# One core, five engines, one hand-sized list: a new order of work for a GateLoop block and a maxout FFN

## The chip, the cores and the metric

The kernel runs on one core of a Trainium2 chip, in one launch. A core has five engines that run side by side, each through its own stream of instructions in order: PE multiplies matrices (the profile lists its weight loads apart, as PEld), DVE works on vectors, ACT computes functions such as exp and sin, POOL does odd jobs and issues some of the transfers, SP only issues transfers. Matrix products land in PSUM, everything else lives in SBUF. The metric is device time in microseconds (us), less is better.

## The reference

Two blocks follow each other. The first is a gated linear recurrence for 4 batches, 8 heads, 768 steps and head dimension 48; the second a feed-forward block on 3072 tokens, width 384, inner width 768:

```python
mag = np.sqrt(a_re * a_re + a_im * a_im)
scale = np.minimum(mag, 0.999) / (mag + 1e-06)
a_re_n, a_im_n = (a_re * scale, a_im * scale)
for t in range(S):
    new_re = ar * S_re - ai * S_im        # ar, ai: row t of a_re_n, a_im_n
    new_im = ar * S_im + ai * S_re
    S_re, S_im = (new_re + outer(k[t], v[t]), new_im)
    y[t] = q[t] @ S_re
x = y.transpose(0, 2, 1, 3).reshape(B * S, H * D)
h = np.maximum(np.maximum(x @ w1, x @ w2), x @ w3)
out = h @ w_out
```

## The kernel before

**Tiling.** The recurrence is not run step by step. It is cut into chunks of 128 steps; a chunk of one batch is one x, and two batches side by side (x and y in the names) make one group g. Six chunks a batch and four batches give 12 groups, 24 x's. Inside a chunk the product of all gates between two steps is written with logarithms of magnitudes (running sums of Ln) and with angles (running sums of turns), so the chunk becomes a masked product of q and k, and a state is carried from chunk to chunk.

**The words.** All work is cut into named words such as `tpqx:8`: the name is the step, x or y the half of the group, the number the group. On PE these are: `cs` and `sums` (running sums of angles and logs), `F` (decays), `tpk` and `tpq` (transposes of k and q), `A` and `B` (scores of a chunk), `dk` (update of the state), `y` (output of the chunk), all of them made of small matmuls; then the FFN: `U` (up projections, x @ (w2 - w1) and x @ (w3 - w1), 9 matmuls of 256 columns), and `P1` to `P7`, `Px`, `Py` (down projection by Strassen's scheme, 7 half-size products instead of 8, and the x @ w1 part folded into one matrix). An f32 matmul is two passes on PE, and each pass is a weight load and a matmul, so one `A` is 128 PE instructions, one `y` 224, one `B` or `F` 64, one `dk` 128, one `U` 36, one `P` 16. On the other engines: gate steps (`sqr`, `add`, `lnL`, `expw`, `lnw`, `mulw`, `turn` and others), angles (`t`, `nf`, `af`, `sa`, `sb`), the products with exp of the sums (`mk`, `uk`, `kEn`, `Q1`, `Q2`, `KB`, `QB`, `QG`), masks (`g0` to `g3`, `b0`, `b1`), state (`h0` to `h3`), and for the FFN `u`, `S1` to `S4`, `r` and `o`. `L...` words are loads, `D` the store.

**Start of the kernel.** The weights come as f64 words and are turned into f32 by hand: `WL` loads a block (12 blocks), `Wa` runs on ACT, `Wb`, `Wc`, `We`, `Wf` on DVE, and `Wg` adds the first weight matrix into a block of the others by an accumulating transfer that POOL issues. `T`, `t`, `M`, `m` fold w1 with w_out. `CL` builds constants (masks) on POOL. The first group's FFN runs in smaller words (`U11x` and so on), before the Strassen factors (`J`) exist.

**What sets the order.** One list, SCHEDULE (line 21), names all 1903 words in the order in which they are issued; a class `Bound` (line 202) ties every instruction of an engine to the one before it on that engine, so the list is the order of each engine. SP and POOL queues get their transfers in the same order. What crosses engines waits on semaphores. SLOTS gives, for each new tile of PSUM, one of four slots of two banks: a PE word that takes a slot waits until the slot's last tile has been read. OTHER names the words that change engine: a load in it goes by POOL's queue instead of SP's, a copy or an absolute value by DVE instead of ACT (`copy` line 242, `magnitude` line 249), and an addition by DVE instead of an accumulating transfer by POOL (`increase` line 256).

**Buffers.** The gate tiles L, w and e of a group have one buffer each; `gates` (line 504) takes all three at the group's first gate word. The result tiles `ot` (line 921) of both halves are taken together at the first of the words that add up results.

Of the kernel before, what the change touches and what calls it, by code (L numbers as in the profile page):

```python
# [31 lines left out]
say:0 atan:1 Wb4:0 Wc2:0 Wg1:0 kEnx:0 Wc4:0 We2:0 Lry:2 Lrx:2 sby:0 sqr:2 g2x:0 sqi:2 M0:0 Wf2:0 WL5:0 M1:0 add:2
uqy:0 lnL:2 expe:2 Bx:0 g3x:0 b0x:0 M2:0 b1x:0 tpqy:0 Qcy:0 m1:0 We4:0 Cdy:0 turn:1 sumsx:1 Eqx:1 uky:0 Wf4:0
tpky:0 Ekx:1 Wg2:0 csy:1 m0:0 Q2y:0 kEny:0 Enx:1 Kcy:0 Q1y:0 mqx:1 ty:1 dkx:0 sumsy:1 h1x:0 h2x:0 nfy:1 relu:2
csx:1 tx:1 mkx:1 QGx:0 Wa5:0 Eqy:1 nfx:1 Eky:1 expw:2 Lvy:0 dky:0 Ay:0 h1y:0 Wb5:0 abs:2 QBy:0 h3x:0 Wc5:0 g0y:0
Liy:3 KBy:0 g1y:0 We5:0 Z2:0 g2y:0 yx:0 g3y:0 WL7:0 Wa7:0 Wb7:0 Eny:1 Wf5:0 xx:0 lne:2 xor:2 Wg4:0 By:0 b0y:0 QGy:0
U11x:0 u11x:0 b1y:0 Fx:1 U01x:0 Z4:0 Wc7:0 half:2 f0x:1 f2x:1 f1x:1 f3x:1 We7:0 addw:2 lnw:2 expL:2 mulai:2 mulw:2
Wf7:0 yy:0 Z3:0 xy:0 u01x:0 U02x:0 h2y:0 h3y:0 Wg5:0 U12y:0 Lqy:1 Lvx:1 Lky:1 afy:1 say:1 U12x:0 stt:2 afx:1 u02x:0
sby:1 WL8:0 u12x:0 Wa8:0 Wb8:0 U11y:0 U01y:0 Cdy:1 Cdx:1 Wg7:0 sbx:1 atan:2 turn:2 Wc8:0 U02y:0 u01y:0 Fy:1 u11y:0
mqy:1 sax:1 f2y:1 f3y:1 f0y:1 f1y:1 We8:0 Wf8:0 u12y:0 u02y:0 U21y:0 csx:2 Lnop:2 tx:2 u21y:0 csy:2 ty:2 uqx:1  # L40
ukx:1 nfx:2 tpqx:1 Qcx:1 Lvx:2 uqy:1 nfy:2 sumsy:2 tpkx:1 Kcx:1 mky:1 Wg8:0 uky:1 tpqy:1 U22y:0 Qcy:1 Lqy:2 kEnx:1
tpky:1 Kcy:1 u22y:0 kEny:1 sumsx:2 Ekx:2 Lkx:2 Q1x:1 mkx:2 Eqy:2 dkx:1 Liy:4 afx:2 Q2x:1 Enx:2 Eky:2 mqy:2 sbx:2
sax:2 QBx:1 Q1y:1 h0x:1 Eny:2 Q2y:1 Oy:0 oy:0 h1x:1 KBx:1 h2x:1 h3x:1 Ax:1 Bx:1 g0x:1 g1x:1 g2x:1 g3x:1 QGx:1 Lqx:2
Lvy:2 Eqx:2 U21x:0 Fx:2 b0x:1 Ay:1 mqx:2 b1x:1 u21x:0 ukx:2 yx:1 U22x:0 Lix:3 sqi:3 f3x:2 f2x:2 J3:0 h0y:1 f1x:2
QBy:1 f0x:2 Lry:3 Lrx:3 sqr:3 add:3 lnL:3 expe:3 relu:3 lne:3 g0y:1 KBy:1 g1y:1 Lvy:1 Lky:2 mky:2 u22x:0 g2y:1
h0x:2 expw:3 abs:3 xx:1 Ox:0 ox:0 QGy:1 g3y:1 By:1 b0y:1 dky:1 b1y:1 uqx:2 addw:3 afy:2 h1y:1 Fy:2 tpkx:2 Kcx:2
h2y:1 h3y:1 f0y:2 xor:3 kEnx:2 Lnop:3 sumsx:3 Lix:4 f3y:2 tpqx:2 Qcx:2 lnw:3 Q1x:2 QBx:2 yy:1 xy:1 f2y:2 dkx:2
Lkx:3 h1x:2 KBx:2 h2x:2 h3x:2 f1y:2 Lqx:3 expL:3 mulw:3 half:3 QGx:2 Enx:3 Lvy:3 Eqx:3 Q2x:2 mulai:3 Ekx:3 Lry:4
U11:1 u11:1 mkx:3 stt:3 Cdy:2 atan:3 U12:1 mqx:3 u12:1 Ax:2 Bx:2 Fx:3 g0x:2 g1x:2 g2x:2 sqi:4 Lrx:4 sqr:4 Lix:5
say:2 g3x:2 Cdx:2 sby:2 U01:1 f3x:3 f2x:3 u01:1 f0x:3 uqy:2 f1x:3 U02:1 Lvx:3 b1x:2 add:4 lnL:4 S3:1 b0x:2 expe:4  # L50
uky:2 turn:3 h0x:3 h0y:2 J1:0 J2:0 tpky:2 Dx:0 Lky:3 u02:1 S1:1 kEny:2 S2:1 Kcy:2 tpqy:2 Qcy:2 yx:2 sumsy:3 xx:2
Lqy:3 Eny:3 Q2y:2 csy:3 Eky:3 ty:3 Eqy:3 nfy:3 csx:3 Q1y:2 tx:3 dky:2 nfx:3 h1y:2 lne:4 relu:4 Fy:3 afx:3 QBy:2
sbx:3 sax:3 h2y:2 J4:0 P5:1 QGy:2 Liy:5 h3y:2 KBy:2 f0y:3 f2y:3 P7:1 P1:1 Dy:0 Ay:2 f3y:3 f1y:3 By:2 P6:1 g0y:2
g1y:2 Px:1 g2y:2 S4:1 expw:4 r1:1 ukx:3 g3y:2 mqy:3 abs:4 P2:1 P3:1 b0y:2 b1y:2 yy:2 xy:2 uqx:3 tpqx:3 Lnop:4 r6:1
addw:4 r5:1 r7:1 r57:1 tpkx:3 kEnx:3 lnw:4 Qcx:3 Lry:5 mky:3 expL:4 Lkx:4 Q1x:3 mulw:4 afy:3 say:3 Kcx:3 sby:3 Py:1
P4:1 oy:1 ox:1 U11:2 u11:2 sumsx:4 Ekx:4 xor:4 Lrx:5 sqr:5 QBx:3 QGx:3 mulai:4 KBx:3 mkx:4 Fx:4 dkx:3 Dx:1 h1x:3
Lvy:4 U01:2 Eqx:4 Q2x:3 half:4 h2x:3 Enx:4 sqi:5 f2x:4 h3x:3 f3x:4 Cdx:3 Dy:1 Bx:3 uqy:3 u01:2 Ax:3 g0x:3 stt:4
Cdy:3 Lqx:4 g1x:3 g2x:3 g3x:3 h0y:3 Lvx:4 b1x:3 f1x:4 U02:2 add:5 u02:2 S3:2 mqx:4 b0x:3 U12:2 f0x:4 h0x:4 atan:4
uky:3 tpky:3 tpqy:3 Kcy:3 yx:3 Qcy:3 turn:4 csx:4 u12:2 kEny:3 S1:2 csy:4 tx:4 sumsy:4 xx:3 Eky:4 Q2y:3 nfx:4 dky:3
Q1y:3 Eny:4 Eqy:4 h1y:3 h2y:3 ty:4 nfy:4 h3y:3 lnL:5 relu:5 KBy:3 sbx:4 Lqy:4 P1:2 afx:4 sax:4 QBy:3 P7:2 Ay:3 By:3  # L60
g0y:3 Py:2 Lry:6 Lkx:5 QGy:3 g1y:3 Liy:6 g2y:3 expw:5 Px:2 P5:2 Lrx:6 r1:2 P4:2 S2:2 S4:2 P6:2 P2:2 ukx:4 g3y:3
uqx:4 expe:5 lne:5 b1y:3 mqy:4 r6:2 r5:2 P3:2 b0y:3 r7:2 r57:2 yy:3 afy:4 Fy:4 oy:2 say:4 sby:4 f2y:4 f3y:4 tpkx:4
Lnop:5 Kcx:4 ox:2 uqy:4 f0y:4 f1y:4 xy:3 Lky:4 mky:4 kEnx:4 tpqx:4 Qcx:4 abs:5 sqr:6 Lix:6 Q1x:4 Dy:2 U11:3 dkx:4
u11:3 xor:5 sumsx:5 QBx:4 Lvy:5 Eqx:5 h1x:4 Ekx:5 half:5 QGx:4 addw:5 lnw:5 Cdx:4 Enx:5 Q2x:4 KBx:4 h2x:4 mkx:5
expL:5 mulw:5 Fx:5 mulai:5 h3x:4 f3x:5 Dx:2 f0x:5 f2x:5 f1x:5 U01:3 u01:3 sqi:6 stt:5 atan:5 uky:4 add:6 lnL:6
U02:3 Cdy:4 Ax:4 u02:3 g0x:4 g1x:4 g2x:4 Lqx:5 g3x:4 h0y:4 Bx:4 mqx:5 b0x:4 b1x:4 Lqy:5 U12:3 tpky:4 expe:6 turn:5
# [5 lines left out]
kEnx:5 QBx:5 QGx:5 Lkx:6 Enx:6 Dy:3 h0x:5 Q2x:5 U01:4 Eqx:6 f2x:6 u01:4 mulw:6 mulai:6 stt:6 U02:4 u02:4 f0x:6
uky:5 mkx:6 f1x:6 S3:4 Ax:5 f3x:6 Bx:5 atan:6 sqi:7 add:7 lnL:7 U11:4 u11:4 Lqy:6 U12:4 Lqx:6 mqx:6 expe:7 half:6
turn:6 g0x:5 g1x:5 g2x:5 g3x:5 Lix:8 b0x:5 tpky:5 Lvx:6 b1x:5 lne:7 Dx:3 tpqy:5 u12:4 S1:4 kEny:5 Kcy:5 sumsy:6
dkx:5 Qcy:5 h1x:5 Liy:8 Eny:6 Q2y:5 KBy:5 csx:6 tx:6 Eqy:6 S2:4 csy:6 Eky:6 ty:6 nfy:6 yx:5 P5:4 Lrx:8 P7:4 Q1y:5
QBy:5 nfx:6 h0y:5 Ay:5 g0y:5 xx:5 g1y:5 afy:6 By:5 say:6 sby:6 dky:5 h1y:5 S4:4 relu:7 g2y:5 g3y:5 P1:4 Lvy:6 sbx:6
r1:4 afx:6 sax:6 expw:7 Px:4 b0y:5 QGy:5 P6:4 P2:4 r6:4 Py:4 Lnop:7 mqy:6 r5:4 uqy:6 r7:4 r57:4 P3:4 b1y:5 yy:5
abs:7 uqx:6 ukx:6 addw:7 ox:4 tpqx:6 Lky:6 Lry:8 tpkx:6 mky:6 Qcx:6 sqr:8 kEnx:6 P4:4 Kcx:6 xy:5 Fy:6 oy:4 dkx:6
Q1x:6 Dy:4 f0y:6 f1y:6 QBx:6 QGx:6 f2y:6 sumsx:7 Q2x:6 f3y:6 uky:6 Ekx:7 Enx:7 Dx:4 h1x:6 h2x:6 xor:7 h3x:6 lnw:7
expL:7 Eqx:7 mulai:7 KBx:6 half:7 Fx:7 f3x:7 f2x:7 U11:5 Lkx:7 u11:5 U01:5 u01:5 f0x:7 f1x:7 Ax:6 g0x:6 mulw:7  # L80
# [958 lines left out]
```

## Time and profile before

| what | us |
|---|---|
| device time, three runs | 570.74, 571.22, 572.38 (median 571.22) |
| profiled execution, from its first instruction to its last (its span) | 567.5 |
| PE busy with matmuls | 529.4 (93%) |
| weight loads (beside the matmuls) | 452.3 (80%) |
| DVE busy | 480.7 (85%) |
| ACT busy, of it 55 table loads | 395.0 (70%), 70.6 |
| POOL busy | 168.3 (30%) |

The trace of the profiled execution holds its own time as the span; what lies around it is not in it, and the median of the runs is 3.7 us above the span. A line of a timeline gives start and length in us, engine, operation, what is written and read, and in brackets the idle time ahead of it and what ended that. "issue" there means that the engine waited for nothing that the profile shows. All instructions carry line 211, the helper inside `Bound` that issues them, so they are told apart by their tiles.

### The profile page before, as it was taken

To read this page: it belongs to the slowest core of one execution; us is meant where nothing else is said; L and a number is where in the kernel's file an instruction comes from. 1 tells how busy PE (TensorE), PEld (TensorE's weight loads), DVE (VectorE), ACT (ScalarE), POOL (GpSimd) and SP (SyncE) were. 2 spreads that over 40 slices of the span, in tenths; PEclk is the share of its full clock that TensorE was granted. 3 is DMA by queue.
4 is the path that set the end of the run, shared out by engine and by line. 5 is a ranking of instruction groups with operands and counts; after the bars stand their busy time and mean duration, and the time that the engine had idled before them with its cause. 6 is when DMAs were issued, how large, how long until landed. Compare 5 with 4: busy or idle time off the path is not lost.

```text
span 567.5 us, 22834 instructions
## 1 busy us (share of the span) xinstructions
PE 529.4 (93%) x10086; PEld 452.3 (80%) x10086; DVE 480.7 (85%) x762; ACT 395.0 (70%) x677; POOL 168.3 (30%) x257
## 2 busy tenths in 40 slices
...
GB/s 256 250 173 143 217 148 131 112 85 46 90 96 54 78 79 89 75 100 71 61 70 73 88 70 38 66 69 111 26 122 36 83 48 55 3 30 2 2 29 28
...
## 3 DMA queue, kind: packets, MB, share of 16 engines
...
q0 software_dynamic: 10864, 16.37, 15.8%
q8 instruction: 79, 1.29, 0.9%
...
## 4 chain that ended last, share of the span: by engine, by line
PE 59%; issue 11%; DVE 6%; DMA 4%; POOL 2%; ACT 2%; DVEq 0%; POOLq 0%; ACTq 0%
PE up L211 23%; PE op L211 17%; PE y L211 5%; PE A L211 3%; PE tp L211 3%; PE dk L211 3%; DMA w<-L 2%; PE sums L211 2%; PE cs L211 2%; PE F L211 1%; DMA q<-in_q_dram 1%; DVE w L211 1%; ACT L L211 1%; PE B L211 1%; DMA Ln<-e 1%
## 5 line engine op out<-in xcount | busy, mean ns | idle before, releaser
L211 PE MATMUL up<-xhx,w 128*128 128x256 f32 x792 | 178.0, 382 | 1.0 <-ACT En L211 0.5
L211 PEld LDWEIGHTS up<-xhx,w 128*128 128x128 f32 x792 | 148.4, 190 | 22.1 <-ACT En L211 0.9
L211 ACT ACT_TABLE_LOAD x55 | 70.6, 1283 | 1.7 <-PEq L1023 0.8
L211 POOL DMA_DIRECT2D ar<-nf x40 | 35.4, 1295 | 79.7 <-DVE ar L211 79.7
L211 PE MATMUL op<-wo,xhx 128*128 128x192 f32 (+1 forms) x220 | 48.3, 361 | 0.0
L211 DVE TENSOR_TENSOR Q<-Q,f 112x1024 f32<-112x1024 f32 (+1 forms) x48 | 45.4, 951 | 2.9 <-ACT Q L211 2.8
L211 POOL DMA_DIRECT2D Ln<-e x10 | 10.1, 1013 | 124.8 <-ACT Ln L211 71.8
L211 ACT COPY atm<-B 32x128 f32<-32x128 f32 x96 | 24.6, 256 | 25.2 <-DVE atm L211 23.6
L211 ACT ACTIVATE f<-F 48x232 f32<-48x232 f32 x96 | 34.4, 359 | 10.3 <-DVE g L211 3.5
L211 POOL DMA_DIRECT2D k<-in_k_dram x52 | 36.1, 857 | 17.2 <-DVE uk L211 16.9
L211 PE MATMUL y<-QG,g 112*32 112x64 f32 x1408 | 38.5, 219 | 2.8 <-issue 2.8
L211 DVE TENSOR_TENSOR ot<-ot,op 128x192 f32<-128x192 f32 (+1 forms) x66 | 27.1, 417 | 16.4 <-PE op L211 12.0
L211 PE MATMUL y<-atm,vb 128*32 128x64 f32 x1152 | 39.4, 221 | 1.0 <-issue 0.5
L211 POOL DMA_DIRECT2D q<-in_q_dram x52 | 38.7, 1197 | 0.3 <-DVE uq L211 0.3
L211 PEld LDWEIGHTS op<-wo,xhx 128*128 128x128 f32 x220 | 36.6, 190 | 2.5
L211 PEld LDWEIGHTS y<-QG,g 112*32 112x32 f32 x1408 | 34.9, 109 | 3.1 <-issue 3.1
L211 PEld LDWEIGHTS y<-atm,vb 128*32 128x32 f32 x1152 | 32.6, 109 | 5.8 <-issue 4.0
L211 DVE TENSOR_TENSOR xhx<-xhx,up 128x768 f32<-128x768 f32 x22 | 20.9, 951 | 18.5 <-PE up L211 17.6
L211 POOL DMA_DIRECT2D vb<-in_v_dram x44 | 31.9, 1037 | 8.4 <-PE y L211 5.2
L211 PE MATMUL op<-wo,strassen 128*128 128x192 f32 x176 | 33.2, 332 | 0.0
L211 PE MATMUL A<-Q,K 112*32 112x80 f32 x1536 | 31.6, 234 | 1.3 <-DVE Q L211 0.7
L211 ACT ACTIVATE xhx<-up 128x768 f32<-128x768 f32 x20 | 16.2, 812 | 23.8 <-PE up L211 23.6
...
## 6 DMA issues: line engine op xcount, KB each, us to landing
...
```

The lines of the kernel that those rows point to most:

```text
L211: ins = f(*a, **kw)
```

## The change

All three lists are replaced. Both SCHEDULE lists hold the same 1903 words, in another order. The new one runs `CL` before any load of q and k, puts the first group's x half ahead of its y half, and spreads the FFN words of PE otherwise. Before, PE's words fall into 53 stretches of FFN words with 53 stretches of small ones between; after, 52 and 52, and a stretch of small words has most often 3 or 4 words, where before 2 or 3 were most common and up to 8 occurred (the start apart). SLOTS is a new assignment of the same 304 tiles. OTHER has 76 words instead of 60: 32 instead of 23 copies, absolute values, maxima and additions on DVE that would else be ACT's or POOL's, and 44 load words on POOL's queue instead of 37 (each four transfers), the rest of them on SP's.

Three pieces of code change with it. A gate tile is taken at the first word that writes it (`sqr` takes e, `sqi` takes L, `expw` takes w). P2 and P3 may come in either order: the one that comes second ends the sum. The two result tiles are taken one by one, at the first word that writes each.

```diff
@@ -19,123 +19,122 @@
 SCHEDULE = """
-Zf:0 Zg:0 Lrx:0 sqr0:0 Lix:0 sqi0:0 add0:0 Lry:0 sqr1:0 Liy:0 xor0:0 lnL0:0 expe0:0 expw0:0 sqi1:0 add1:0 xor1:0
-relu0:0 WL0:0 lne0:0 Wa0:0 Lnop0:0 abs0:0 Wb0:0 half0:0 Wc0:0 We0:0 lnL1:0 expw1:0 WL3:0 Wa3:0 Wb3:0 expe1:0 lne1:0
-WL6:0 Wf0:0 pw0:0 relu1:0 Wc3:0 lnw0:0 expL0:0 mulw0:0 Lnop1:0 WL10:0 sumsx:0 Eqx:0 Wa6:0 T0:0 abs1:0 t0:0 Fx:0
-f3x:0 f1x:0 f0x:0 mulai0:0 We3:0 Wb6:0 Ekx:0 stt0:0 Wc6:0 Wf3:0 Enx:0 pw1:0 sumsy:0 lnw1:0 expL1:0 We6:0 Eny:0
-WL9:0 Lix:1 f2x:0 mulw1:0 mulai1:0 Lry:1 Lqy:0 Lqx:0 mqx:0 Wf6:0 WL11:0 atan0:0 stt1:0 Wa9:0 Wa10:0 turn0:0 Lkx:0
-Wb9:0 mkx:0 half1:0 Lvx:0 Wc9:0 Wb10:0 atan1:0 turn1:0 csx:0 Liy:1 Lrx:1 tx:0 nfx:0 WL1:0 Wc10:0 We9:0 sqi:1 sqr:1
-add:1 We10:0 Wf10:0 Wf9:0 afx:0 sax:0 sbx:0 uqx:0 csy:0 ty:0 Lix:2 Eky:0 Lky:0 mky:0 Liy:2 Eqy:0 Lqx:1 mqy:0 Wa1:0
-T1:0 Wb1:0 lnL:1 ukx:0 xor:1 tpqx:0 Qcx:0 tpkx:0 Q2x:0 Wa11:0 Wb11:0 t1:0 relu:1 QBx:0 Kcx:0 expw:1 Wc1:0 expe:1
-abs:1 Fy:0 Wc11:0 f2y:0 T2:0 CL:0 f0y:0 f1y:0 Lkx:1 Q1x:0 KBx:0 pw:1 WL2:0 lne:1 WL4:0 f3y:0 nfy:0 We11:0 lnw:1
...
-nfx:9 S2:7 expe:10 Eky:9 yx:8 P7:7 Q2y:8 nfy:9 P5:7 P6:7 Q1y:8 QBy:8 xx:8 Lrx:11 sbx:9 afx:9 sax:9 ukx:9 QGy:8
-lne:10 S4:7 relu:10 xor:10 Lnop:10 Fy:9 Lry:11 By:8 f0y:9 f2y:9 Ay:8 g0y:8 f1y:9 f3y:9 P1:7 Lvy:9 g1y:8 g2y:8 g3y:8
...
+Lrx:0 sqr0:0 Lix:0 sqi0:0 add0:0 Zf:0 CL:0 Zg:0 lnL0:0 Lry:0 sqr1:0 expw0:0 Liy:0 sqi1:0 WL3:0 add1:0 WL0:0 expe0:0
+lne0:0 WL9:0 relu0:0 lnL1:0 expe1:0 Wa3:0 expw1:0 xor1:0 relu1:0 xor0:0 Lnop0:0 abs0:0 half0:0 Wb3:0 lne1:0 pw0:0
+Wc3:0 We3:0 Wa0:0 Lnop1:0 WL6:0 Wf3:0 lnw0:0 expL0:0 Lry:1 mulai0:0 Wb0:0 Wa9:0 sumsx:0 T1:0 abs1:0 pw1:0 mulw0:0
+Wc0:0 stt0:0 Liy:1 We0:0 atan0:0 Wb9:0 Lix:1 turn0:0 lnw1:0 Wc9:0 Wf0:0 expL1:0 csx:0 We9:0 Ekx:0 mulw1:0 tx:0 Wa6:0
+WL1:0 Enx:0 nfx:0 Wb6:0 Fx:0 Eqx:0 Lqx:0 mulai1:0 WL10:0 f0x:0 Wc6:0 f1x:0 T0:0 WL11:0 mqx:0 afx:0 stt1:0 f2x:0
+atan1:0 We6:0 sax:0 Lkx:0 t0:0 mkx:0 sbx:0 Wf6:0 T2:0 half1:0 Lky:0 Lrx:1 Wf9:0 Wa10:0 uqx:0 ukx:0 f3x:0 Wb10:0
+turn1:0 Wa11:0 Wb11:0 sqi:1 Wc10:0 tpkx:0 tpqx:0 Qcx:0 t1:0 Wc11:0 Liy:2 Lqy:0 csy:0 sumsy:0 Kcx:0 We10:0 Q2x:0 sqr:1
+ty:0 Wf10:0 We11:0 add:1 nfy:0 QGx:0 WL2:0 t2:0 Wa1:0 Eny:0 Wf11:0 lnL:1 Wb1:0 kEnx:0 expw:1 WL4:0 Eky:0 mky:0 QBx:0
+relu:1 expe:1 Lix:2 abs:1 Fy:0 f2y:0 Eqy:0 f3y:0 f1y:0 lne:1 f0y:0 M0:0 pw:1 Q1x:0 Wc1:0 xor:1 mqy:0 We1:0 Wa2:0 Lry:2
...
+f1x:9 Dy:6 u02:7 f2x:9 U12:7 uqx:9 tpkx:9 u12:7 f3x:9 f0x:9 tpqx:9 Cdy:9 Bx:8 S1:7 b1x:8 KBy:8 b0x:8 QBy:8 Ay:8 Kcx:9
+yx:8 g0y:8 g1y:8 g2y:8 g3y:8 Qcx:9 P1:7 P5:7 xx:8 sumsy:9 S3:7 Fy:9 r1:7 S2:7 QGy:8 mulai:10 By:8 b1y:8 Q1x:9 Eqy:9
...
 """
 
 SLOTS = """
...
 OTHER = set("""
-Lqx:0 Lkx:0 Lvx:0 Lky:0 Lkx:1 Lqy:2 Lqx:2 Lvy:1 Lky:2 addw:3 Lkx:3 Lqx:3 Lvy:3 Lky:3 Lvy:4 Lqx:4 Lvx:4 xx:3 Lkx:5
-afy:4 xy:3 Lqx:5 Lqy:5 Lky:5 xx:4 abs:6 Lkx:6 Lqy:6 Kcx:6 u01:5 Lqy:7 Lky:7 Lnop:8 Lvx:8 Lqy:8 Lky:8 xx:7 Lvy:8
-addw:9 Lkx:9 Lqy:9 xx:8 Lvy:9 abs:10 Lkx:10 Lqx:10 afx:10 Lvy:10 Lqy:10 Kcx:10 xy:9 addw:11 Lvx:11 xx:10 afy:11
-Lvy:11 Qcx:11 Qcy:11 xy:11 u11:11
+abs0:0 Lqy:0 Lqx:0 Lkx:0 Lky:0 Lqx:1 Lvy:0 Lqy:1 Lky:1 Lqy:2 Lqx:3 Lvy:3 Lvx:3 Lky:3 Lqy:3 Lkx:4 Lvy:4 Lqx:4 Lqy:4
+Lky:4 Lvy:5 Kcy:4 Lvx:5 Lky:5 Lkx:6 u01:4 Lqy:6 Lqx:6 Lnop:7 addw:7 Lky:6 u11:5 u01:5 Lqx:7 Lvx:7 Qcy:6 Lqy:7 Lvy:7
+abs:8 Kcx:7 Lkx:8 u01:6 Lvx:8 Lqy:8 Qcy:7 Lky:8 xx:7 afy:8 Lvy:8 Lnop:9 Kcy:8 Lqx:9 Lqy:9 Qcy:8 xx:8 Lvy:9 abs:10
+Lkx:10 u11:8 Lqx:10 afx:10 Lvy:10 Lky:10 afy:10 Lqy:10 xy:9 Lkx:11 u11:9 Kcy:10 afy:11 Kcy:11 u11:10 Qcy:11 xx:11
+u11:11 u01:11
 """.split())
...
@@ -506,7 +505,8 @@
         if name not in names.split():
             return False
         lo, hi = cs[0] * DM, (cs[-1] + 1) * DM
-        for nm in "Lwe":
+        nm = {"sqr": "e", "sqi": "L", "expw": "w"}.get(name)
+        if nm:
             once((nm, g), lambda: nat1.tile([P, W], FP, tag=nm, name=nm))
 
         def part(nm):
@@ -910,23 +910,28 @@
         if name[0] == "P" and name[1:].isdigit():
             i = int(name[1:])
             left = {1: a11, 2: a12, 3: s1, 4: a22, 5: s1, 6: s2, 7: s3}[i]
+            last = i not in (2, 3) or ("op7", g, "half") in T
+            if i in (2, 3):
+                T["op7", g, "half"] = i
             for n in range(4):
                 mm(out=r[i], lhsT=left[:, n], rhs=factor(i)[:, (n + 2 * (g % 2)) % 4],
-                   start=i in (1, 5, 6, 7) and n == 0, stop=i != 2 and n == 3)
+                   start=i in (1, 5, 6, 7) and n == 0, stop=last and n == 3)
         elif name in ("Px", "Py"):
             c = "xy".index(name[1])
             x0 = features(g)[:, 2 * (g % 2), c * P:(c + 1) * P]
             mm(out=ps[:, c, 0:DM], lhsT=x0, rhs=wx[:, 0], start=True, stop=False)
         else:
-            ot = [once(("ot", g * C + c), lambda: fp2.tile([P, DM], FP, tag="ot", name="ot")) for c in range(C)]
-            xl, xr, yl, yr = (ot[c][:, h * NH:(h + 1) * NH] for c in range(C) for h in range(2))
+            def part(c, h=None):
+                ot = once(("ot", g * C + c), lambda: fp2.tile([P, DM], FP, tag="ot", name="ot"))
+                return ot if h is None else ot[:, h * NH:(h + 1) * NH]
+
             if name == "r1":
-                act.copy(out=xl, in_=r[1])
+                act.copy(out=part(0, 0), in_=r[1])
             else:
-                out, in0, in1 = {"r6": (yl, xl, r.get(6)), "r5": (xr, yl, r.get(5)), "r7": (yl, yl, r.get(7)),
-                                 "r57": (yr, yl, r.get(5)), "ox": (ot[0], ot[0], ps[:, 0, 0:DM]),
-                                 "oy": (ot[1], ot[1], ps[:, 1, 0:DM])}[name]
-                dve.tensor_tensor(out=out, in0=in0, in1=in1, op=OP.add)
+                to, of, add = {"r6": ((1, 0), (0, 0), r.get(6)), "r5": ((0, 1), (1, 0), r.get(5)),
+                               "r7": ((1, 0), (1, 0), r.get(7)), "r57": ((1, 1), (1, 0), r.get(5)),
+                               "ox": ((0,), (0,), ps[:, 0, 0:DM]), "oy": ((1,), (1,), ps[:, 1, 0:DM])}[name]
+                dve.tensor_tensor(out=part(*to), in0=part(*of), in1=add, op=OP.add)
 
     def project(x, name):
 
```

More of the change, by code (lines that the diff above doesn't have):

```diff
@@ L32 @@
[L32 to L66, printed above, removed]
@@ L72 @@
[L72 to L80, printed above, removed]
-stt:7 atan:7 g1x:6 g2x:6 Lqx:7 Lix:9 sqi:8 g3x:6 mqx:7 add:8 Bx:6 Cdy:6 b0x:6 lnL:8 expe:8 U12:5 U02:5 Lvx:7 b1x:6
@@ L87 @@
-f1y:7 f3y:7 Enx:8 f2y:7 Q1x:7 Dy:5 QBx:7 QGx:7 KBx:7 mulai:8 Ekx:8 Lkx:8 mkx:8 Eqx:8 half:8 Q2x:7 U11:6 u11:6 U01:6
-u01:6 h0x:7 dkx:7 h1x:7 h2x:7 f0y:7 h0y:7 Cdx:7 Fx:8 Dx:5 f2x:8 f0x:8 Ax:7 f3x:8 g0x:7 f1x:8 g1x:7 h3x:7 U02:6
-sqi:9 add:9 g2x:7 stt:8 Cdy:7 atan:8 lnL:9 relu:9 U12:6 Bx:7 Lqx:8 mqx:8 u02:6 g3x:7 Lvx:8 b1x:7 b0x:7 S3:6 tpqy:7
-turn:8 u12:6 S1:6 tpky:7 kEny:7 Lqy:8 S2:6 Kcy:7 h0x:8 csx:8 Liy:10 tx:8 nfx:8 KBy:7 csy:8 ty:8 nfy:8 Qcy:7 Q2y:7
-yx:7 sumsy:8 Eny:8 Eky:8 dky:7 Eqy:8 Q1y:7 QBy:7 Lky:8 xx:7 h1y:7 h2y:7 P5:6 afx:8 Ay:7 g0y:7 g1y:7 g2y:7 g3y:7
@@ new lines @@
+tpky:0 Kcy:0 Ekx:1 Fx:1 csx:1 tx:1 f0x:1 lne:2 yx:0 xx:0 Enx:1 Eqx:1 Lkx:1 Q2y:0 f2x:1 nfx:1 Lvx:1 Q1y:0 csy:1 Z4:0
+xor:2 Wg2:0 Ay:0 QBy:0 WL5:0 KBy:0 Wa5:0 Wb5:0 Lqy:1 f3x:1 g0y:0 afx:1 kEny:0 g1y:0 expw:2 U01x:0 Wg4:0 f1x:1 u01x:0
+sax:1 abs:2 Wc5:0 g2y:0 Lvy:0 ty:1 QGy:0 g3y:0 U11x:0 u11x:0 We5:0 Lky:1 By:0 b1y:0 b0y:0 dky:0 h1y:0 sbx:1 mkx:1 yy:0
+Wf5:0 nfy:1 sumsy:1 WL7:0 Wa7:0 afy:1 addw:2 xy:0 U02x:0 lnw:2 ukx:1 mqx:1 U11y:0 Wg5:0 Eky:1 half:2 Cdx:1 h2y:0 Wb7:0
+h3y:0 Wc7:0 Fy:1 Eny:1 u02x:0 expL:2 Cdy:1 Eqy:1 WL8:0 Liy:3 tpkx:1 We7:0 mulw:2 f0y:1 Wf7:0 mulai:2 U12x:0 f2y:1
@@ new lines @@
+Kcx:1 U12y:0 Wa8:0 Z3:0 f3y:1 u12x:0 Lnop:2 U01y:0 stt:2 Wb8:0 uqx:1 Wg7:0 Lvy:1 f1y:1 atan:2 turn:2 Lqx:3 say:1
+U02y:0 Wc8:0 u01y:0 sby:1 u02y:0 We8:0 tpqx:1 u11y:0 Qcx:1 mky:1 Wf8:0 csx:2 tx:2 nfx:2 csy:2 U21y:0 kEnx:1 ty:2
+u21y:0 mqy:1 Lix:3 u12y:0 Wg8:0 uqy:1 U21x:0 afx:2 uky:1 sumsx:2 dkx:1 nfy:2 Enx:2 Lky:2 Q2x:1 u21x:0 Q1x:1 KBx:1
+tpky:1 h0x:1 tpqy:1 QBx:1 Ekx:2 Eqx:2 Qcy:1 U22y:0 u22y:0 afy:2 Ax:1 Kcy:1 say:2 g0x:1 g1x:1 h1x:1 Liy:4 Bx:1 g2x:1
+g3x:1 b1x:1 Lkx:2 Oy:0 sqi:3 h2x:1 sbx:2 Fx:2 b0x:1 mkx:2 sby:2 sax:2 QGx:1 oy:0 h0y:1 kEny:1 KBy:1 Lqx:2 h3x:1
@@ new lines @@
+sumsy:2 Eqy:2 dky:1 mqx:2 uqx:2 Eny:2 Eky:2 f0x:2 ukx:2 f3x:2 U22x:0 f1x:2 f2x:2 tpkx:2 Lry:3 h1y:1 Q1y:1 tpqx:2
+u22x:0 Lrx:3 sqr:3 Q2y:1 Qcx:2 Kcx:2 QBy:1 yx:1 add:3 xx:1 Ay:1 QGy:1 lnL:3 expw:3 Lqy:2 relu:3 expe:3 abs:3 addw:3
+g0y:1 g1y:1 g2y:1 By:1 mqy:2 mky:2 uky:2 g3y:1 h2y:1 lne:3 Ox:0 uqy:2 Fy:2 h3y:1 ox:0 Q2x:2 tpqy:2 Lix:4 tpky:2 b1y:1
+Q1x:2 J3:0 b0y:1 Lry:4 yy:1 Lrx:4 Kcy:2 xor:3 Ax:2 QGx:2 h0x:2 Lnop:3 xy:1 half:3 Cdy:2 Lvx:2 lnw:3 expL:3 Qcy:2 f3y:2
+Cdx:2 mulw:3 Dx:0 sqr:4 kEny:2 kEnx:2 Lkx:4 g0x:2 f1y:2 U11:1 mulai:3 g1x:2 U12:1 stt:3 Lvy:2 u11:1 U01:1 QBx:2 Lkx:3
```

125 lines of the change are left out of this document (79 added, 46 removed).

## The prediction

> **What bounds the kernel now.** I read the busy line first, then the chain, then busy time by stretches, then the gaps of PE.
>
> ```profile
> PE 529.4 (93%) x10086; PEld 452.3 (80%) x10086; DVE 480.7 (85%) x762; ACT 395.0 (70%) x677; POOL 168.3 (30%) x257
> PE 59%; issue 11%; DVE 6%; DMA 4%; POOL 2%; ACT 2%; DVEq 0%; POOLq 0%; ACTq 0%
> q8 instruction: 79, 1.29, 0.9%
> ```
>
> PE is the bound by its share and by the chain that ended last. The third line is the queue that brings the instructions themselves; its meaning comes below.
>
> ```profile
> 0.00:20.00 20.00, 8.99 (x78) 4.59 (x78) 15.96 (x37) 16.96 (x36) 15.85 (x44) 1.00 0.93 262
> 20.00:40.00 20.00, 8.03 (x89) 5.88 (x90) 17.31 (x29) 15.50 (x24) 14.19 (x20) 0.56 0.86 175
> 60.00:80.00 20.00, 15.93 (x473) 12.94 (x475) 18.07 (x30) 15.76 (x34) 6.51 (x9) 0.91 1.01 217
> 480.00:520.00 40.00, 40.00 (x837) 35.66 (x836) 34.72 (x55) 19.25 (x37) 0.00 (x0) 1.00 0.04 13
> ```
>
> These are busy times by stretch (PE, PEld, DVE, ACT, POOL, then PE's granted clock, the DMA share, GB/s). There are two regimes. Up to 80 us PE is half idle and DVE is the full engine. From 80 us on PE is busy without a break and DVE has some 4 us in 40 to spare.
>
> I then took each PE word's time from its first matmul to the next word's, wherever nothing waited: U 3.98 us, P 1.30, y 1.72, A 1.13, dk 0.87 to 1.05, tp 0.54, cs and sums 0.7 each, F 0.49, B 0.41. They add up to 512.5 us for the old list and 511.9 for the new one; the rest of the old span is 3.4 after PE's end and 51.6 of waits. The word U12y, the first of the FFN that had to wait for a weight block, starts 37.5 us later than the PE work ahead of it takes; the other 14 us build up in 480 us. Of these, five belong to the word boundaries themselves, and the rest are real stops, of two kinds. One kind:
>
> ```profile
> 70.49 0.28 PE L211 MATMUL y<-QG,g 112*32 112x64 f32 x2
> 72.38 0.26 PE L211 MATMUL y<-QG,g 112*32 112x64 f32 x3 [1.61 <-issue]
> ...
> 194.00 1.08 PE L211 MATMUL dk<-vb,uk 64*64 64x48 f32 x60
> 195.67 0.29 PE L211 MATMUL dk<-vb,uk 64*64 64x48 f32 x4 [0.58 <-issue]
> ...
> 254.66 0.24 PE L211 MATMUL y<-QG,g 112*32 112x64 f32 x1 [1.14 <-issue]
> ```
>
> PE stops in the middle of a word, waiting for nothing. There are six such stops (also at 77, 111 and 126 us). Counting PE's instructions in the trace (weight loads, matmuls and its 157 own waits and drains), the first one after each stop is number 1217, 1473, 2753, 3521, 6337, 8641: always 193 more than a multiple of 256. The instruction queue moved 79 packets, 1.29 MB, so 16 KB each, and 79 x 256 = 20,224 is PE's instruction count. So PE stops at the edge of a block of 256 that has not come yet. A packet starts some 1.4 us (late in the kernel) after PE is 40 instructions short of an edge, and PE passes the next edge 2.4 to 2.8 us after the packet's start. Hence a block, counted with the 40 instructions ahead of it, must take PE 3.85 us after 256 us of the kernel and about 4.5 before, when the transfers are denser; what it takes less is a stop. Among the old blocks after 85 us none is shorter than 3.77 us. Laid over the old list, edges and the words' times give 2.9 us of stops after 85 us; the trace has 3.2 (0.32, 0.73, 0.80, 1.35, from instruction to instruction).
>
> **The change part by part.** *Blocks of instructions.* The small words are the fast ones: A and then y are 352 instructions in 2.85 us. In the old list group 8's y half of B, its A, and the y of its x half lie apart, with P words between; the new list has Bx:8, Ay:8, yx:8 in a row, and an edge falls into Ay:8, so that the next block holds only A and y and takes 2.37 us with its lead. It must take 3.85, so 1.5 us are lost. I laid the edges over the whole new list with the old words' times: 19 blocks come out under 4 us, 14 of them after 256 us with 2.3 to 3.0 us, and the stops add up to 24.5 us. The place of the edges depends on how many waits of its own PE gets, of which the old trace has 157 and the new list is not known to have the same: edges 16 instructions earlier give 30.4, 16 later 17.8, and over all 256 places the sum lies between 8.6 and 32.6. For the old list the same scan has its least value just where its edges lie. I take 24.2, the mean of the three near places, and keep both ends. The old list's own 3.2 go: +21.0.
>
> [...]
>
> *The start.* DVE has the same work ahead of the weight blocks in both lists: back to back (a 768-wide operation starts 0.87 us after the one before), Wf5 is 62.9 us into DVE's list before and 63.2 after. Of its gaps, one goes:
>
> ```profile
> 30.60 0.96 DVE L211 CUSTOM_DVE_ANT_0 L<-L,e 128x768 f32<-128x768 f32 x1 [2.66 <-ACT e L211]
> ...
> 20.45 5.95 POOL L211 TENSOR_SCALAR_AFFINE_SELECT KB<-KB 128x128 f32<-128x128 f32 x2
> ...
> 82.93 3.25 PE L211 MATMUL up<-xT,w 128*128 128x128 f32 x27 [0.50 <-DMA w<-w]
> ```
>
> The first line waited for group 1's gates, loaded behind weights; the new list asks for three of their four parts earlier and does that step 8 us of DVE work later: -2.7. Against it, CL moves ahead of the loads of q and k on POOL. In the trace those loads begin at 7.3 us, and CL (second line its slowest part) takes 12.8 us. Then Lqx:0 would be issued from 20.1, its fourth transfer 1.9 later, landing 5.8 after that: 27.8, where DVE wants q at 23.6 and k at 25: +4.8 for both, and nothing if CL is as fast as its first select (0.40 us against 5.48 for its twin), for then it ends near 13. The nearest row is CL itself, so I take 4.8: the weights come 2 us later or not at all. The third line shows what PE then waits for: block 5's accumulating transfer (Wg5, about 7.8 us from Wf5's end). The new list has 47.3 us of PE work ahead of that point instead of 45.4. So PE is between 6.4 us less behind (no delay) and 1.8 less behind (whole delay). With CL's whole price: -2.0, ends -6.4 and +3.
>
> [...]
>
> *Work that changes engine.* Nine more operations on DVE, and one more accumulating transfer on POOL, by the words moved: 10.3 us more on DVE (a copy of K or Q 1.22 there, 1.02 on ACT; a maximum 0.95), about 0.9 us a group where DVE has 4 idle in 40. Taken at 0; without that cover it costs up to 9.6. ACT changes its function table at 59 places instead of 55, 4 x 1.28 = 5.1 us, hidden by 30% idle. POOL issues 28 more transfers at 0.61 us, 17 us on an engine that is 30% busy; what is queued behind a load that waits there are the accumulations of Ln and w, which ACT reads several us later. SP gets as many fewer. Taken at 0, ends -2 and +4.
>
> *Buffers, flags, slots.* Taking tiles later adds no instruction; P2 and P3 only move their flags. The smallest distance between a tile's last PE work and its slot's next use is 0.5 to 1.3 us in the new list, 0.9 to 1.4 in the old: 0, ends 0 and +1.
>
> *Boundaries.* An FFN word ahead of a small one costs 0.09 us more, behind one 0.10. 53 stretches become 52: -0.2.
>
> *Other stops.* Waits for data cost PE some 4.6 us after 100 us (the longest 1.0, tpky:3 for its uk). In the new list scores follow their transposes after 18 us of PE work (median) instead of 12, so there is more slack, and 24 us of stops give every other engine more time: -3, ends -4.6 and +3.
>
> The sum: +24.2 - 3.2 - 2.0 + 0 + 0 - 0.2 - 3.0 = +15.8, against the profiled execution 567.5 + 15.8 = 583.3. The runs' median lies 3.7 above its span, which I carry over: 587.0.
>
> **The rivals.** *The edges fall kindly.* If PE's own waits shift the edges by 64 instructions, the stops are 8.6 instead of 24.2: 567.5 + 8.6 - 3.2 - 2.0 - 0.2 - 3.0 = 567.7, so 571.4, no change; with the start's whole gain of 6.4 it is 567.0. For it speaks that nothing fixes the new count of waits; against it, that 64 of 157 is much, and that no place gives less than 8.6.
>
> *Blocks come in time.* One mechanism on the other side: PE could keep several blocks ahead, and the six stops could have another cause, such as DMA traffic at these moments. Then nothing is paid, and what is left is -3.2 - 2.0 - 0.2 - 3.0: 559.1, so 562.8. It decides if blocks of 2.5 us pass without a stop. Against it speak six stops out of six at the same place in a block; that no old block is that short leaves it open. [...]
>
> *The start is late as well.* POOL's queue, with CL ahead of q and k, delays DVE by 5 us and the weights are not ready for it: +3 instead of -2, and the stops at 30: 567.5 + 30.4 - 3.2 + 3 - 0.2 = 597.5, so 601.
>
> **How the numbers follow.** Main case 0.70 (stops of 12 to 30 us: 574 to 594), kindly placed edges 0.10, blocks in time 0.12, late as well 0.08. Predicted is the main case, 587.0, its own range 574 to 594. The range of 8 in 10 cuts most of the third and the end of the fourth: 568 to 599. A measurement tells 0.3% (1.7 us) from no change. Faster are the third case and a third of the second (0.14), same 0.06, slower 0.80.
>
> **What would show it.** Right: gaps of 1 us and more put down to issue inside y, A, dk, F words, some 15 to 20 of them, each at the 193rd instruction of a block or at one common other number; PE busy about 515 to 530 while the span grows; DVE's and ACT's shares falling. For the start: q's transfers issued on POOL after 13 to 20 us, DVE waiting for q or k near 24, and U12x near 80. Wrong: no gaps put down to issue in rows of Ay and yx; or PE waiting for uk, g or w instead, which would make the moved work the cause.

## The result and the profile after

| | before | after |
|---|---|---|
| device time, median of four runs, us | 571.61 | 586.66 (584.91 to 589.58) |
| span of the profiled execution, us | 567.5 | 585.8 (its device time 587.79) |
| PE's stops at block edges after 60 us | 9, in sum 6.5 | 20, in sum 25.9 |
| PE's waits for data of over 0.4 us after 60 us | 16, in sum 9.0 | 12, in sum 7.6 |
| time at a granted clock of 0.50 after 60 us | 3.4 | 6.8 |

The change makes the kernel slower: 1.0267 times the time before, 95% interval 1.0233 to 1.0301. 587.0 had been forecast.

The last three rows of the table are counted from the trace up to the last matmul, and the experiments use the same counts. PE's instructions are numbered in order of start; a stop at an edge is a step of more than 0.25 us from one start to the next that leads to an instruction whose number is 193 more than a multiple of 256. 0.06 us is taken off each for the step itself. A wait for data is any other step of more than 0.4 us to an instruction that has a semaphore to wait for, less the same 0.06 us. The granted clock is the share of full speed at which PE was allowed to run.

First the busy line, the chain and the instruction queue, from the page of the changed kernel:

```profile
PE 532.2 (91%) x10086; PEld 453.8 (77%) x10086; DVE 490.6 (84%) x771; ACT 391.3 (67%) x671; POOL 184.3 (31%) x286
q8 instruction: 79, 1.29, 0.9%
PE 74%; issue 7%; POOL 6%; DMA 5%; ACT 5%; DVE 3%; SPq 0%; POOLq 0%; DVEq 0%; ACTq 0%
```

PE does the same 10,086 matmuls, 2.8 us busier in sum, in a span that is 18.3 us longer: what grew is mostly PE's idle time. The busier part has a place too: after 60 us the clock was granted at 0.50 from 73.4 to 76.8 us before the change, and from 86.5 to 89.9 and from 134.3 to 137.7 us after it. DVE has 9.9 us more work and yet a smaller share. The chain's "issue" share fell from 11 to 7%, so that number isn't a meter of the stops. The waits of PE are a better one. Here are all rows of that view whose releaser is "issue" (us in total, times, longest), first of the kernel before, then of the changed one.

```profile
PE y L211 <- issue: 3.3, 3, 1.6
PE dk L211 <- issue: 0.6, 1, 0.6
PE F L211 <- issue: 0.4, 1, 0.4
```

```profile
PE A L210 <- issue: 4.3, 3, 2.0
PE up L210 <- issue: 3.0, 2, 2.6
PE sums L210 <- issue: 2.5, 1, 2.5
PE B L210 <- issue: 2.3, 2, 1.3
PE dk L210 <- issue: 1.7, 2, 0.9
PE y L210 <- issue: 1.3, 2, 0.9
PE F L210 <- issue: 1.1, 1, 1.1
PE tp L210 <- issue: 1.0, 2, 0.5
PE cs L210 <- issue: 1.0, 2, 0.5
PE op L210 <- issue: 0.7, 1, 0.7
```

They had been 4.3 us, most of it in y; in the changed kernel ten kinds of words have 18.9 us. That no one kind carries them fits a cause that lies in the position in the stream, not in the data. Single stops, from the timeline of PE:

```profile
70.11 0.48 PE L210 MATMUL A<-Q,K 112*32 112x80 f32 x14 [1.99 <-issue]
...
133.22 2.13 PE L210 MATMUL up<-xhx,w 128*128 128x256 f32 x7 [2.64 <-issue]
...
316.48 0.55 PE L210 MATMUL sums<-Ln,rest 64*64 64x192 f32 x7 [2.53 <-issue]
...
455.24 0.61 PE L210 MATMUL A<-Q,K 112*32 112x80 f32 x21 [1.25 <-issue]
...
543.65 0.74 PE L210 MATMUL A<-Q,K 112*32 112x80 f32 x27 [1.06 <-issue]
```

Each falls into the middle of a word. Numbered, the first instructions after them are 1217, 3777, 10945, 16321, 19649: again 193 more than a multiple of 256. In the quiet part after 256 us there are 14 such stops of 0.6 to 2.8 us, and the trace shows why: the packet of the instruction queue for block 63 starts 1.03 us after PE is 40 instructions short of the edge, the next edge is passed 2.72 us after that start, and the block with its lead had only 2.26 us of work. All 20 stops of the changed kernel end 2.2 to 2.7 us after the start of their packet, and in the fourteen traces of this case none of 1108 edges is passed sooner than 2.17 us after it. That is the sign of a stop that the packet ends.

The count has two soft places. Two of the 20 stops, those at 86 us (2.5) and 503 us (1.0), the profile puts down to data (DVE's w and ACT's Q) that came at about the same time as the block, so they might have occurred without an edge. And three of the nine in the kernel before, at 116, 245 and 341 us (1.3 us in sum), ended 3.7 to 6.7 us after their packet's start; the packet doesn't explain those.

The start, in the timelines of DVE and POOL:

```profile
25.45 0.56 DVE L210 TENSOR_TENSOR q<-E,q 128x384 f32<-128x384 f32 x1 [2.01 <-DMA q<-in_q_dram]
...
29.19 0.56 DVE L210 TENSOR_TENSOR k<-E,k 128x384 f32<-128x384 f32 x1 [1.85 <-DMA k<-in_k_dram]
```

```profile
15.69 1.40 POOL L210 MEMSET atm<- 128x512 f32 x2
17.04 3.08 POOL L210 DMA_DIRECT2D q<-in_q_dram  x4
20.11 2.54 POOL L210 DMA_DIRECT2D k<-in_k_dram  x4
```

`CL` ends at 17, the loads of q and k are issued behind it, and DVE waits 3.9 us for the two. U12x starts at 87.1 us, 39.8 behind the PE work ahead of it (37.5 before), of which the three edges at 70, 78 and 86 us take 5.6 (2.3 before).

By stretches (same columns as in the prediction):

```profile
60.00:80.00 20.00, 14.03 (x479) 11.58 (x483) 16.43 (x26) 17.35 (x36) 12.48 (x17) 1.00 0.87 174
480.00:520.00 40.00, 39.08 (x815) 34.35 (x814) 33.57 (x55) 22.14 (x38) 0.00 (x0) 1.00 0.13 28
```

In the last one PE is no longer busy without a break: the 0.92 us that are missing are the stop at 503 us. The same columns for the spell of low clock behind the stop at 133 us:

```profile
134.30:137.70 3.40, 3.40 (x9) 2.69 (x8) 2.73 (x5) 0.00 (x0) 3.40 (x7) 0.50 0.51 109
```

Eight matmuls of `up` follow each other there at 0.42 us each, where they follow at 0.22 us at a clock of 1.00. Before the change the spell begins 1.0 us behind the end of the stop of 1.8 us at 72 us; in the changed kernel the two begin 0.8 and 1.1 us behind the stops of 2.5 and 3.0 us that end at 85.8 and 133.2 us, and there is none behind those of 2.2 and 2.8 us that end at 70.1 and 316.5 us. What sets them was not tried. By an estimate from the two paces such a spell can make a stop cost more than its own length, by at most half the spell.

### The profile page after: what moved, and what is told of

Same layout as the page of the kernel before. It is cut to its first block, busy times and chain, and to the rows that moved or that the text cites. A ratio compares the mean times of both kernels' runs of the same rounds, so it can differ in the third digit from the quotient of the medians.

```text
span 585.8 us, 22787 instructions
## 1 busy us (share of the span) xinstructions
PE 532.2 (91%) x10086; PEld 453.8 (77%) x10086; DVE 490.6 (84%) x771; ACT 391.3 (67%) x671; POOL 184.3 (31%) x286
## 4 chain that ended last, share of the span: by engine, by line
PE 74%; issue 7%; POOL 6%; DMA 5%; ACT 5%; DVE 3%; SPq 0%; POOLq 0%; DVEq 0%; ACTq 0%
PE up L210 29%; PE op L210 22%; PE y L210 6%; PE A L210 4%; PE tp L210 3%; PE dk L210 3%; PE cs L210 3%; PE sums L210 2%; DMA w<-w 2%; POOL q L210 1%; PE B L210 1%; PE F L210 1%; DMA k<-in_k_dram 1%; DMA w<-L 1%; POOL KB L210 1%
## 5 line engine op out<-in xcount | busy, mean ns | idle before, releaser
L210 PEld LDWEIGHTS up<-xhx,w 128*128 128x128 f32 x792 | 149.7, 191 | 25.9 <-issue 3.9
L210 POOL DMA_DIRECT2D q<-in_q_dram x72 | 48.8, 766 | 64.8 <-DVE uq L210 61.9
L210 POOL DMA_DIRECT2D k<-in_k_dram x56 | 37.3, 801 | 48.0 <-DVE uk L210 42.3
L210 ACT ACTIVATE f<-F 48x232 f32<-48x232 f32 x96 | 34.4, 358 | 11.8 <-PE F L210 7.9
L210 PEld LDWEIGHTS y<-atm,vb 128*32 128x32 f32 x1152 | 32.6, 109 | 5.6 <-issue 3.6
L210 POOL DMA_DIRECT2D w<-L x9 | 9.4, 1045 | 80.5 <-ACT L L210 51.0
L210 PEld LDWEIGHTS A<-Q,K 112*32 112x32 f32 x1536 | 27.9, 110 | 6.6 <-issue 4.9
L210 PE MATMUL op<-w,strassen 128*128 128x192 f32 x176 | 32.3, 330 | 0.0
```

The costliest lines, as they stand in the source:

```text
L210: ins = f(*a, **kw)
```

## The experiments

The rival to the blocks was that the new order costs by waits for data or by work on other engines, and that the stops are something that happens to fall there. The test needed is one that moves the edges and leaves the order alone. PE's first matmul starts at 7.84 us before the change and at 7.36 after it, so tiny matmuls can be put ahead of it that shift every later edge and cost next to nothing (a whole block of them: ratio 1.0017). To forecast them I took the instruction times of the two traces, took the stops out, and laid edges at other places over them.

**1, 2, 3 and 5: shifted edges.** The edit, with 22, 50, 14 and 64 matmuls (four PE instructions each):

```diff
                 ps = T["pw", g, lo] = banks("pw")
+                for _ in range(22 if (g, cs[0]) == (0, 0) else 0):
+                    mm(out=ps[0:3, 1, 0:3], lhsT=biases[:, 0:3], rhs=biases[:, 0:3], start=True, stop=True)
```

The kernel before, shifted by 88 instructions:

> The kernel before, with 22 tiny matmuls (3 columns of constants, 88 PE instructions with their weight loads) ahead of PE's first word, where PE waits until 7 us anyway. They shift every edge of 256 instructions by 88 against the work and change nothing else. Theory (stops at block edges): the old list laid under the shifted edges has 16 to 20 us of stops instead of 0.5 to 2, so 585 to 590 us, stops at the same place in a block, 193 as before. Rival (the order of the words and their waits for data set the time): 571 to 573. Rival (the added instructions themselves cost): under 1 us, since they end before 7 us.

The changed kernel, shifted by 200:

> The changed kernel with 50 tiny matmuls (200 PE instructions) ahead of PE's first word. Theory: the changed list has its least stops near this place of the edges, 3.5 to 5.3 us instead of 17 to 22 by the same reckoning, so 570 to 575 us. Rival (the new order costs by its waits for data or by the engine work it moves): 586 to 588.

The changed kernel, shifted by 56:

> The changed kernel with 14 tiny matmuls (56 PE instructions) ahead of PE's first word, the worst place of the edges by the same reckoning: 31 to 37 us of stops instead of 17 to 22. Theory: 597 to 603 us. Rival (order, waits, moved work): 586 to 588.

The kernel before, shifted by a whole block:

> The kernel before with 64 tiny matmuls (256 PE instructions, one whole block) ahead of PE's first word. Theory (stops at block edges): the edges lie again where they lay against the work, so the time is that of the kernel before, 569 to 572 us, though nearly three times as much was added as in the run with 88. Rival (the added instructions, or any shift, cost): 584 or more.

| kernel | shift | time, us | ratio to before | span | stops at edges, number and sum | us at clock 0.50 after 60 us |
|---|---|---|---|---|---|---|
| before | 0 | 569.9 to 571.6 in the series | 1 | 567.5 | 9, 6.5 | 3.4 |
| before | 88 | 583.71 | 1.0235 [1.0208, 1.0262] | 582.6 | 18, 21.2 | 3.4 |
| before | 256 | 571.11 | 1.0017 [0.9981, 1.0052] | 566.5 | 8, 7.0 | 0 |
| after | 0 | 586.66 | 1.0267 [1.0233, 1.0301] | 585.8 | 20, 25.9 | 6.8 |
| after | 56 | 594.76 | 1.0447 [1.0403, 1.0491] | 593.4 | 24, 30.2 | 6.8 |
| after | 200 | 574.90 | 1.0085 [1.0054, 1.0116] | 571.4 | 7, 7.1 | 10.2 |

The timeline of PE in the kernel before shifted by 88 has stops where it had none:

```profile
1.05 1.24 PE L211 MATMUL pw<-biases 128*3 128x3 f32 x44 [1.05 <-DVE biases L211]
...
73.35 0.64 PE L211 MATMUL A<-Q,K 112*32 112x80 f32 x25 [2.52 <-issue]
78.97 0.43 PE L211 MATMUL B<-QB,KB 112*32 112x32 f32 x11 [2.95 <-issue]
...
246.02 0.44 PE L211 MATMUL A<-Q,K 112*32 112x80 f32 x10 [1.13 <-issue]
```

The first line is all that was added: 1.24 us, done before 3 us. The same list of words is then 2.3% slower, and in every one of these kernels the stops lie at instruction 193 of a block, so they moved through the work with the edges. A whole block's shift changes nothing. And the new order loses most of what it lost: 11.8 of 15.1 us go by a shift alone. Span less stops is 561.0, 561.4, 559.5, 559.9, 563.2 and 564.3 in the order of the table: within 5 us for times that differ by 25. The granted clock is no rival for the 88: its spells have the same 3.4 us with and without the shift. It explains part of the 5 us: with half of the time in the last column taken off too, five of the six lie between 559.2 and 559.8, and the new order without a shift at 556.5. My ranges lay too high at the two slow ones (585 to 590 against 583.7, 597 to 603 against 594.8) and held at the others.

**4: the code without the lists.** The changed code with the three old lists.

> The code of the changed kernel with the three lists of the kernel before. Theory (the lists alone make the difference; the buffers taken later add no instruction): 570 to 573 us. Rival (the buffers taken at first use add waits on PE or elsewhere): above 574.

569.96 us, ratio 0.9999 [0.9977, 1.0021]. Taking tiles at first use and moving the flag from P3 to the later of the two costs nothing; it only allows other orders.

**6: what a block costs by itself.** The last `Ay` is computed 21 times over:

```diff
-            for h in range(H):
+            for h in list(range(H)) * (21 if x == NX - 1 else 1):
```

> The kernel before, with the last Ay computed 21 times over into the same tile: 20 x 128 PE instructions more of the fastest kind, near the end of the kernel, where the transfers are few. By the A words of the trace they take 20 x 1.13 = 22.6 us. Theory (PE holds one block ahead at most): 10 more edges, at each a block with its lead of 40 instructions takes 2.6 us where 3.45 to 3.85 are needed, so stops of about 0.9 to 1.2 us at each and 31 to 35 us more in all, 601 to 606 us. Rival (several blocks are held ahead, and the stops come from transfers or waits): 22 to 24 us more, 592 to 595.

605.75 us (one run), 35.1 more than before. In the timeline of PE:

```profile
517.55 2.42 PE L211 MATMUL A<-Q,K 112*32 112x80 f32 x128 [1.33 <-issue]
521.02 2.42 PE L211 MATMUL A<-Q,K 112*32 112x80 f32 x128 [1.05 <-issue]
524.76 2.42 PE L211 MATMUL A<-Q,K 112*32 112x80 f32 x128 [1.32 <-issue]
528.24 2.42 PE L211 MATMUL A<-Q,K 112*32 112x80 f32 x128 [1.05 <-issue]
531.98 2.42 PE L211 MATMUL A<-Q,K 112*32 112x80 f32 x128 [1.32 <-issue]
535.45 2.42 PE L211 MATMUL A<-Q,K 112*32 112x80 f32 x128 [1.05 <-issue]
```

128 matmuls and their 128 weight loads are one block: 2.42 us busy, 1.05 or 1.32 idle, again and again, with the DMA engines 2% busy from 517 to 550 us. So in a run of fast blocks PE gets one every 3.47 to 3.75 us (4.02 for the last): the packet starts 1.0 to 1.2 us after an edge is passed, and the next edge is passed 2.3 to 2.7 us after that. Ten edges, ten stops, in sum 13.6 us; the first edge of the run stops PE like the others, though PE had 8.4 and 4.2 us for the two blocks before the one that ends there. Had several been held ahead, as the rival had it, the first edges would have passed. A single short block can pass: in the changed kernel shifted by 200 the one that ends at 159 us takes 1.73 us without a stop, because PE had been slow around the edge before it (4.6 us from 40 instructions ahead of that edge to the next one).

**7: `CL` behind the loads.** On the changed kernel shifted by 200, so that stops cover less:

```diff
-Lrx:0 sqr0:0 Lix:0 sqi0:0 add0:0 Zf:0 CL:0 Zg:0 ...
+Lrx:0 sqr0:0 Lix:0 sqi0:0 add0:0 Zf:0 Zg:0 ...
-... Wf6:0 T2:0 half1:0 ...
+... Wf6:0 T2:0 CL:0 half1:0 ...
```

> The changed kernel with 200 PE instructions ahead, and CL moved from behind Zf:0 to behind T2:0 in the list, so that POOL issues the first loads of q and k ahead of it. Theory of the prediction's start (CL holds up q and k by 3.9 us of DVE time, of which the weights pass on up to that): the two DVE waits near 23 and 27 us go, and the time falls by 1 to 4 us from 574.9, to 571 to 574. Rival (hidden behind the weights or the block edges): 574 to 576.

575.91 us against 574.90 without the move: no gain. DVE's waits for q and k near 25 and 28 us (1.3 and 0.7 in the kernel shifted by 200) are gone, but POOL issues the accumulating transfer Wg4 at the same time, 64.8 us against 64.6, U11x, which reads that block, starts at 73.36 against 73.54, and U12x at 87.3 instead of 86.2. The stops came out 3.1 us longer (10.2) and PE's waits for data 2.7 longer, while 6.8 us less were spent at a clock of 0.50, so a gain of some 2 to 3 us can't be excluded by the time alone; the start of U12x speaks against it.

**8, 9 and 10: the work that changes engine.** The changed kernel shifted by 200, with OTHER of before, whole, its load words alone, and its compute words alone.

> The changed kernel with 200 PE instructions ahead, and the list OTHER of the kernel before: nine operations fewer on DVE, seven load words back on SP's queue. The prediction took this moved work at 0: 573 to 577 us. Rival (DVE's 10 us more, or the transfers on POOL, cost): 566 to 572.

> The changed kernel with 200 PE instructions ahead and the load words of the old OTHER alone (37 on POOL's queue in place of 44), the 32 compute words as changed. The whole old OTHER costs 24 us here, against the prediction's 0. Theory A (the loads: a load back in SP's queue stands behind that queue's waits in the new order and comes late): 590 to 600 us. Theory B (the nine operations back on ACT and POOL cost, since they stand in queues placed for DVE): 573 to 577.

> The changed kernel with 200 PE instructions ahead, the 44 load words as changed, and the 23 compute words of the old OTHER. Theory A (the loads alone cost): 573 to 577 us, as with the new compute words. Theory B (the operations back on ACT and POOL cost): 590 to 600.

599.18, 584.23 and 592.05 us against 574.90. Here my expectation failed clearly: the whole costs 24.3 us. Of the split, theory B gave the right number for the compute words and the wrong one for the loads: both halves cost (17.2 and 9.3). PE's waits for data are 30.1, 15.9 and 25.7 us instead of 11.4, the stops at edges 6.7, 11.7 and 5.0 instead of 7.1, and the time at a clock of 0.50 is 20.9, 13.7 and 23.9 us instead of 10.2. So about half of what the loads alone cost are longer stops at edges, 4.6 us; the rest of the three prices is mostly waits for data and the low clock behind them. One place of each, first the old loads (DVE, then PE), then the old compute words:

```profile
404.35 0.56 DVE L209 TENSOR_TENSOR k<-E,k 128x384 f32<-128x384 f32 x1 [5.04 <-DMA k<-in_k_dram]
...
409.44 2.07 PE L209 MATMUL up<-xhx,w 128*128 128x256 f32 x5 [3.14 <-DVE g L209]
```

```profile
199.90 0.56 DVE L209 COPY xhx<-y 128x384 f32<-128x384 f32 x1 [4.41 <-PE y L209]
...
203.00 2.31 PE L209 MATMUL A<-Q,K 112*32 112x80 f32 x61 [3.17 <-DVE Q L209]
```

In the first `Lkx:9`, back on POOL's queue, comes 5 us late for DVE: POOL issues it at 399.0 us, behind an accumulation of Ln that had waited 15.4 us for ACT. PE then waits for what DVE does behind it. In the second a copy of y (`xx:3` and `xy:3` are in the old OTHER) stands on DVE ahead of work on Q, and DVE, in order, waits 4.4 us for y with Q's work behind it. The words of A that follow take 2.31 us for 61 matmuls, against 1.31 for 64 elsewhere: the clock is granted at 0.50 from 202.3 to 209.2 us. So OTHER belongs to its order: the same operation is free in one place of a queue and costs several us in another.

**11 and 12: a better order at the same edges.** Six FFN words in each list, moved a few PE words later, and their slots with them, so that edges no longer fall into runs of small words. A part of the second:

```diff
-... U02:2 U12:2 tpky:3 tpqy:3 yx:3 csx:4 ...
+... U02:2 tpky:3 tpqy:3 yx:3 U12:2 csx:4 ...
```

(PE's words only.)

> The changed kernel, nothing added, with six FFN words moved behind one or two small words (U01:3, U12:4, P2:7 with P3:7, U12:9, U01:10), so that four edges no longer fall into runs of small words alone (the blocks that end at 283, 435, 503 and 527 us). Theory (stops at block edges come from the order of the words against the edges): 4 to 5 us of stops go, 581 to 584 us against 586.7, with no gap at these four edges. Rival (the stops belong to these times or transfers, not to the order): 586 to 588.

> The kernel before with six FFN words moved behind one to three small words (U12:2, U12:3, P3:4, U12:6, U12:7, U02:9), chosen so that no block after 85 us has less than 4 us of work. Theory: 1 to 2 us of the old list's stops go, 568 to 570 us where the kernel before has 570.5. Rival (the stops left in the old list come from fetches that start late, whatever the block holds; or the moved words make the small ones late): 570 to 573.

594.89 us against 586.66, ratio to before 1.0446 [1.0405, 1.0487], and 591.33, ratio 1.0368 [1.0328, 1.0409]: both far slower, where a gain was forecast. The part on the edges came out: in 11 the four edges, at 283, 435, 503 and 527 us in the changed kernel, have steps of 0.05, 0.00, 0.14 and 0.00 us where there had been 0.7 to 1.5, and the stops sum to 18.7 instead of 25.9; in 12 to 3.7 instead of 6.5. But PE's waits for data are 20.3 and 25.6 us instead of 7.6 and 9.0, and 17.1 us in each are spent at a clock of 0.50. The profile of 12 is of its fastest run, 586.11 us. In 12, PE and DVE after the first word moved:

```profile
179.79 3.19 PE L209 MATMUL up<-xhx,w 128*128 128x256 f32 x14
186.72 0.76 PE L209 MATMUL tp<-ident,uk 64*112 64x64 f32 x16 [3.74 <-DVE uk L209]
...
185.62 0.95 DVE L209 TENSOR_TENSOR uk<-CS,k 128x768 f32<-128x768 f32 x1
```

U12:2 takes 4 us, and it had lain between U02:2 and tpky:3. With it there, tpky:3 had waited 1.0 us for its uk, the longest wait of that kind; without it, PE waits 3.74. The FFN words are what covers the way of small ones through DVE and ACT, so a list can't be mended for the edges alone. No version of the new order here beats the kernel before: the nearest is the new order shifted by 200, 0.85% slower.

## Why the prediction was right, point by point

*The blocks, +24.2 less 3.2.* Right in cause and place, a fifth too large. (PE's instruction count is 20,329, not 20,224; the 79 packets are the blocks behind the first 193 instructions.) The edges that the forecast listed, all after 100 us, took 20.3 us where 24.2 were given, and the old list's after 85 us are 4.2: +16.1 instead of +21.0. Of the 4.2 the packets explain 3.0, close to the 3.2 of the forecast. The 14 blocks under 4 us after 256 us are 14 stops. The size was off in more than one way. Five blocks before 256 us had been listed, and there are three stops from 100 to 256 us. And 3.85 us was taken for a block with its lead, and at these 14 edges PE passed 3.2 to 3.9 us after it was 40 instructions short of the edge ahead in all but two, 3.7 in the middle. How the 3.9 us divide between the two is open. The example was the poorest: the edge at 417 us among Bx:8, Ay:8 and yx:8 was given 1.5 us and has 0.6. The bounds came near: shifted to its best and its worst place the list has 7.1 and 30.2 us of stops, and the scan over all places had said 8.6 to 32.6. What had no term are the edges at 70, 78 and 86 us, which took 5.6 instead of 2.3: +3.3, of which the one at 86 us may be a wait for DVE.

*The start, -2.0.* About right, by two terms that were both too large. `CL` took 9.8 us, not 12.8, q was issued at 17.0, not 20.1, and the two waits are 3.9 instead of 4.8. Without the edges (5.6 and 2.3) U12x is 34.2 us behind instead of 35.2: -1.0. In experiment 7 the delay on POOL's queue goes and the weights come no earlier, so CL's price in this term was not on the path there. That U12x would start near 80 us was wrong by 7 us, by the edges ahead of it and 1.9 more of PE work.

*Work that changes engine, 0.* The number fits the change as made, since the terms measured leave nothing over for it; no run shows it by itself, and its reason was wrong. I had argued from DVE's 4 idle us in 40 and ACT's 30%; by that, putting the operations back should be free as well, and in experiment 10 it costs 17 us. Idle share says that an engine could take the work, not that the queue has its operands at that place.

*Buffers, 0.* Right (experiment 4). *Boundaries, -0.2.* No run shows this term by itself. By the forecast's own word times the new list has 511.9 us of work instead of 512.5, so -0.6 goes into the sum below.

*Other stops, -3.* Right in sign, about half the size: PE's waits for data fell from 9.0 to 7.6 us, and behind the start, after 88 us, from 5.3 to 3.6: -1.7. Whether the later scores or the time that stops give the other engines did it was not tried.

*The clock, no term.* From U12x on, 6.2 us were spent at a granted clock of 0.50, where the old kernel had none after its U12y: up to +3.1 by the estimate above.

*The sum.* 583.3 was forecast for the span, 585.8 came, with +16.1 + 3.3 - 1.0 - 0.6 - 1.7 + 3.1 = 19.2 by these counts for a growth of 18.3. The forecast carried 3.7 us from the span to the time; the profiled execution has 2.0, and the median lies 1.1 below its time. That 587.0 and 586.66 are so close is in part luck, since errors of some 1 to 5 us in single terms cancel: the blocks were put too high, the edges before 100 us and the clock had no term. Of the rivals, "blocks come in time" fell with experiment 6, and "edges fall kindly" is what a shift by 200 makes of this list.
